# Sigmoid attention feeding a top-1 mixture of experts: the SyncE queue asks for raw weights and the last two pairs in other steps

## The chip, the cores and the metric

The kernel runs on one core of a Trainium2 chip, as one launch. The metric is the device time of the launch in microseconds (us), lower is better. A core has five engines with an instruction stream each: PE (TensorE), DVE (VectorE), ACT (ScalarE), POOL (GpSimd) and SP (SyncE). Nearly all DMAs of this kernel are issued by SP, whose queue takes them strictly in program order: where one DMA has to wait for a buffer, everything behind it on SP waits too.

## What is computed

Eight batches of 448 tokens with twelve heads of width 64 go through a sigmoid attention; its output, as 3584 token rows of 768, goes through a mixture of eight experts, of which each token takes the one with the largest gate logit.

```python
scores = scale * np.matmul(q, k.transpose(0, 1, 3, 2)) - np.log(S)
attn = 1.0 / (1.0 + np.exp(-scores))
x = np.matmul(attn, v)                    # then (B*S, H*D)
logits = x @ w_gate;  expert_idx = np.argmax(logits, axis=1)
for e in range(E):
    mask = expert_idx == e
    h = np.maximum(x[mask] @ w1[e], 0.0)
    out[mask] = gate_w[mask, None] * (h @ w2[e])
```

## The kernel before

**Attention in phases.** Heads are taken in pairs, six pairs to a batch, two pairs at a time. `attention()` runs 168 steps `s`; 21 steps (`PB`) are a phase `ph`, one batch, and `r` is the step within the phase. A step makes the scores of one seventh of two pairs (8 matmuls of L589, then two sigmoids on ACT) and the weighted sums of the step two before (8 matmuls of L604). So the two pairs whose scores begin at r = 0, 7 and 14 need their values at r = 2, 9 and 16. Pair `g` belongs to phase `g // 6`.

**Dense blocks.** Behind step r = 1 of a phase stands the expert block of batch `b = ph - 2`: all 448 tokens of the batch through the expert that most of them took (`moe`, L229 and L248, 288 matmuls). For batches 1 to 5 (`LEFT`) the block stands in an If (L786, L787) on `whole`, which says whether more than 240 tokens took that expert. Where they did not, the other arm runs, which has no matmuls. Tokens that no block covers are gathered into items at the end. In these inputs seven of the eight blocks run; the one of batch 4, at the start of phase 6, does not.

**What SP does in a late phase.** Phases 3 to 7 from r = 2 on are called `late`. There SP issues, in the order of the program:
- `vn`, the values of a pair (`load_values`, 224 KB, one DMA for an even pair, two for an odd one), into four buffers, at r = 1, 4, 8, 11, 15 and 18. The ones at r = 8, 15 and so on wait for the L604 matmuls that release a buffer;
- `wst`, raw tiles of the next block's weights (L180, 384 KB each) into a ring of five. `wts.load(n)` makes sure that n are asked for; `FIRST` holds the steps. From r = 18 (`SPLIT`) `wts.ahead` splits the first three in two parts on DVE and asks for one more raw tile for each;
- `kn` and `qn`, keys and queries of a pair (`load_pair`, L496, eight DMAs of 56 KB in runs of 128 B), into four buffers. `turn` (L559) transposes them on DVE before the scores can use them;
- `g_tok` (L413, one DMA of 448 single words to DRAM, gate letter "w" at r = 13) and its way back, `g_blocks` (L420, r = 18);
- `x_tok`, token rows of three pairs (`token_rows`, L449, four DMAs of 168 KB to DRAM), at r = 15 and r = 1, once DVE has turned them (`xt`).

In the If, both arms hold the first values, turns and loads of the next pairs (`BESIDE_LOADS`): in the arm with the block they stand between its matmuls, in the other arm one behind the other, 35 DMAs of SP with nothing between them.

All loops are unrolled and the order is the order of the code (`manual_schedule`); a step's loads of weights stand ahead of its matmuls, its `todo` behind them, then the gate steps.

Of the kernel before, what the change touches and what calls it, by code (L numbers as in the profile page):

```python
# [25 lines left out]
def tile_sigmoid_attention_top1_moe(  # L26
# [93 lines left out]
    def gate_columns():  # L120
        nc.gpsimd.tensor_copy(wgp[:, :, 0:E], wg)
# [22 lines left out]
    def raw_view(st, n):  # L144
        return st.rearrange("p (t f) -> p t f", f=n)

    def w2_rows(ereg, r, st):
        d, jh = divmod(r, 2)
        src = w2[bass.ds(ereg, 1), jh * 4 * P : (jh + 1) * 4 * P, d * DW : (d + 1) * DW]
        nc.sync.dma_start(raw_view(st, DW), src.rearrange("e (t p) f -> p (e t) f", p=P))  # L150
# [9 lines left out]
    class Weights:  # L160
# [9 lines left out]
        def load(self, n):  # L170
            while self.loaded < min(n, len(self.eregs) * self.LOADS):
                b, i = divmod(self.loaded, self.LOADS)
                ereg = self.eregs[b]()
                if ereg is None:
                    break
                st = next(raw_ring)
                if i < KF:
                    eng, ereg = (nc.gpsimd, regs["first"]) if b == 0 else (nc.sync, ereg)
                    src = w1[bass.ds(ereg, 1), :, i * P : (i + 1) * P].rearrange("e (t p) f -> p (e t) f", p=P)
                    eng.dma_start(raw_view(st[:, :DM], P), src)  # L180
                else:
                    w2_rows(ereg, i - KF, st)
                self.raw[self.loaded] = st
                self.loaded += 1
# [408 lines left out]
    def weighted(s):  # L593
# [25 lines left out]
    UB = NP // 2  # L619
    PB = UB * ST  # L620
    FIRST = {9: 1, 11: 2, 13: 3, 15: 4, 17: 5}
    SPLIT = PB - 3
    LATE = range(LEFT.start + 2, LEFT.stop + 2)
    TICK = 14
# [14 lines left out]
    LAST = {2: lambda u: load_pair(2 * u + 4), 5: lambda u: load_pair(2 * u + 5)}  # L639
# [24 lines left out]
    }  # L664
    FIRST_LAST = {2: lambda u: load_pair(2 * u + 6), 5: lambda u: load_pair(2 * u + 7)}

    BESIDE_LOADS = {
        2: lambda u: turn(2 * u + 2, "k"),
        3: lambda u: (turn(2 * u + 2, "q"), load_values(2 * u + 2)),
# [7 lines left out]
    def attention():  # L677

        order = ExitStack()
        order.enter_context(tc.manual_schedule())  # L680
        for g in range(2):
            first_pair(g)
        nc.gpsimd.dma_start(wg, w_gate.rearrange("(t p) e -> p t e", p=P))
        load_values(0)
        load_values(1)
        warm_up(WARM)
        first_turn(0)
        first_turn(1)
        for g in (2, 3):
            load_pair(g)  # L690
        for g in (2, 3):
            load_values(g)
        write_blank = blank_records()
        gate_columns()
        pend = {}

        def gate_step(b, what):
            if what == "a":
                gate_a(b)
            elif what == "b":  # L700
                pend[b] = gate_b(b)
            elif what == "c":
                pend[b] = gate_c(b, *pend[b])
                gate_out[b] = pend[b][0]
            elif what == "l":
                load_regs(b)
            elif what == "d":
                gate_d(b, *pend.pop(b))
            elif what == "p":
                put_records(b)  # L710
            elif what == "w":
                put_gates(b)
            elif what == "e":
                gate_e(b)
            elif what == "x":
                while turned:
                    token_rows(*turned.pop(0))
            else:
                for t in range(2):
                    low_half(b, 2 * what + t)  # L720

        ALONE_GATES = {
            3: "a", 4: "b", 6: (0, "c"), 7: (1, "l"), 8: (2,), 12: "d", 18: "w",
        }
        BESIDE_GATES = {
            0: "xa", 1: "b", 3: "c", 4: "l", 5: "w", 6: "d", 7: "p", 8: "e", 11: (0,), 12: (1,), 13: (2,),
        }
        FIRST_GATES = {
            1: "a", 2: "b", 4: "c", 5: "l", 7: "x", 9: "d", 10: "w", 12: (0,), 13: (1,), 14: (2,), 15: "p", 17: "e",
        }  # L730
        LATE_GATES = {
            3: "b", 5: (0, "c"), 6: (1, "l"), 7: (2,), 11: "d", 13: "w", 16: "p", 18: "e",
        }
        ALONE = 2 * PB

        for s in range(N_ST + 2):
            u, i = divmod(s, ST)
            held = ALONE <= s < ALONE + 2
            ph, r = divmod(s, PB)
            late = LATE.start <= ph < LATE.stop and r > 1  # L740
            nb = ph - 1 if late else 0
            if (late or s < ALONE) and r in FIRST and ph:
                wts.load(nb * wts.LOADS + FIRST[r])
            if (late or s < ALONE) and SPLIT <= r and ph:
                wts.ahead(nb * wts.PARTS + r - SPLIT + 1, early=True)
            if s < N_ST and not held:
                scores(s)
            if s >= 2:
                weighted(s - 2)
            if s < N_ST:  # L750
                m = u % UB
                alone = u < 2 * UB - 1
                todo = READY if u < 2 * UB - 2 else LATER if alone or u >= 2 * UB and m else {}
                if i in todo:
                    todo[i](u)
                if u >= 2 * UB and m == UB - 1 and i in LAST:
                    LAST[i](u)
                if u == 2 * UB and i in FIRST_LAST:
                    FIRST_LAST[i](u)
            for what in ALONE_GATES.get(s - PB, ()) if s < ALONE else ():  # L760
                gate_step(0, what)
            for what in LATE_GATES.get(r, ()) if late else ():
                gate_step(nb, what)
            if i in (1, 5) and not ALONE - ST < s < ALONE + 2 or s == ALONE - 5:
                gate_step(None, "x")
            if s == ALONE - 4:
                write_blank()
            elif s == ALONE - 2:
                load_pair(ALONE // ST * 2)
            b, r = divmod(s - 1, PB)  # L770
            b -= 2
            if s == ALONE:
                yield TICK
            if r or b < 0:
                continue
            if b in LEFT:
                u = UB * (b + 2)
                for g in (2, 3):
                    for nm in "kq":
                        turned_tile(2 * u + g, nm)  # L780
                    value_tile(2 * u + g)
                for g in range(2 * u + 4, min(2 * u + 8, NG)):
                    pair_tiles(g)
                rows = list(turned)
                turned.clear()
                whole = nc.values_load(gate_out[b][0:1, 1:2], min_val=0, max_val=1)  # L786
                with tc.If(whole >= 1) as whole_if, tc.manual_schedule():  # L787
                    for tick in range(14):
                        if tick == 0:
                            for at in rows:  # L790
                                token_rows(*at)
                        elif tick in BESIDE_LOADS:
                            BESIDE_LOADS[tick](u)
                        yield TICK
                    yield PER + 1 - 14 * TICK
                with whole_if.Else(), tc.manual_schedule():
                    for at in rows:
                        token_rows(*at)
                    for load in BESIDE_LOADS.values():
                        load(u)  # L800
                gate_step(b + 1, "a")
                continue
            for tick in range(0 if b else 1, 20 if b < B - 2 else 15):
                yield TICK
                for what in (BESIDE_GATES if b else FIRST_GATES).get(tick, ()):
                    gate_step(b + 1, what)
                if b == 0 and tick == 1:
                    gate_e(0)
                elif b == 0 and tick == 2:
                    put_records(0)  # L810
                todo = BETWEEN if b else FIRST_BETWEEN
                if b < B - 2 and tick in todo:
                    todo[tick](UB * (b + 2))
            if b < B - 2:
                yield PER + 1 - 20 * TICK
            if b == 0:
                for n in range(2):
                    scores(ALONE + n)
        order.close()

    wts = Weights([(lambda b=b: regs.get(b)) for b in range(B)])
# [362 lines left out]
```

## Time and profile before

| | before |
|---|---|
| median of 3 runs | 802.11 us (799.76 to 805.47) |
| the profiled execution | 798.6 us |
| its span, from the first to the last instruction | 796.9 us |
| PE busy | 771.9 us (97%) |
| DVE, ACT, POOL busy | 437.1, 376.0, 131.2 us |
| mean granted TensorE clock | 0.985 |
| DMA of SP's queue | 277070 packets, 95.96 MB, 54.1% of 16 engines |

The span is 1.7 us shorter than the time of the same execution. PE is the engine that is nearly always busy, so what matters is where it is not, and where it runs at the lower clock; the page shows both in the 40 slices of the span. Windows over a stage, the timelines of SP, PE and DVE and the chain that ended last then tell what PE waited for.

### The profile page before, as it was taken

The page shows a single profiled execution, that of the slowest core. Times are in us where ns is not written, and L with a number is a line of the kernel's source. Part 1 is how long each engine was busy: PE and PEld are TensorE (multiplying, and loading weights), DVE is VectorE, ACT ScalarE, POOL GpSimd, SP SyncE. Part 2 cuts the span into 40 slices and gives each one's busy share as a digit, 9 for nine tenths or more (in the row PEclk, how much of TensorE's full clock was granted, in tenths as well). Part 3 has the DMA queues.
Part 4 walks back from the last instruction along what each step waited for, and adds up shares of the span by engine and source line. Part 5 has one row for each costly group of instructions (what it writes and reads, how often), then busy time and mean ns, then how long its engine had stood idle before and what let it go on. Part 6 is the DMA issues. An engine that isn't in the chain of part 4 may idle for free.

```text
span 796.9 us, 15247 instructions
## 1 busy us (share of the span) xinstructions
PE 771.9 (97%) x5480; PEld 591.0 (74%) x5480; DVE 437.1 (55%) x932; ACT 376.0 (47%) x681; POOL 131.2 (16%) x201
## 2 busy tenths in 40 slices
PE   9999999999999999999999767999999999999996
PEld 5545898889964899559984323799747998999885
DVE  2475676245447644665436537354375674466763
ACT  6876333863228431573317436442283331335662
POOL 4442305000121002110031001001210223032011
PEclk9999999999999999999999889899999999999999
DMA  8968889567528884288736877884266646688211
GB/s 164 191 144 167 223 173 202 111 141 198 100 47 144 191 227 82 62 155 226 163 68 118 117 165 153 149 219 111 47 112 184 138 111 187 181 283 305 74 37 37
DMA packets 285940, 117.69 MB, mean 148 GB/s; under 512 B 204284, under 2 KB 275980, under 8 KB 285854
## 3 DMA queue, kind: packets, MB, share of 16 engines
q1 hardware_dynamic: 277070, 95.96, 54.1%
q0 software_dynamic: 8352, 19.95, 10.4%
q8 instruction: 47, 0.77, 0.4%
q10 hardware_dynamic: 432, 0.69, 0.3%
q14 instruction: 39, 0.32, 0.2%
HBM read 94.36 MB, written 22.39 MB: 147 GB/s over the span
## 4 chain that ended last, share of the span: by engine, by line
PE 89%; issue 4%; DMA 3%; SPq 2%; DVE 1%; ACT 0%; POOLq 0%; POOL 0%; DVEq 0%
PE ps L248 26%; PE ps L229 25%; PE sc L589 16%; PE av L604 15%; PE ps L1018 2%; PE ps L1046 2%; SPq L496 2%; DMA vn<-in_v_dram 1%; PE psg L284 1%; DMA x_tok<-xt 0%; SPq L449 0%; DMA wst<-in_q_dram 0%; PE pl L300 0%; PE px L950 0%; DMA qn<-in_q_dram 0%
## 5 line engine op out<-in xcount | busy, mean ns | idle before, releaser
L576 ACT ACTIVATE at<-sc,bias_s 128x448 f32<-128x448 f32 x336 | 196.2, 635 | 136.1 <-PE sc L589 133.9
L604 PE MATMUL av<-at,vn 64*64 64x448 f32 x1344 | 192.6, 545 | 5.8 <-DMA vn<-in_v_dram 5.8
L589 PE MATMUL sc<-qt,kt 64*64 64x448 f32 x1344 | 192.6, 554 | 5.4 <-DVE gsum L288 5.4
L589 PEld LDWEIGHTS sc<-qt,kt 64*64 64x64 f32 x1344 | 87.3, 189 | 62.9 <-issue 40.6
L229 PE MATMUL ps<-xh,w1h 128*128 128x448 f32 x336 | 124.2, 370 | 0.3 <-DVE hl L235 0.3
L229 PE MATMUL ps<-xh,w1l 128*128 128x448 f32 x336 | 123.5, 368 | 0.0
L248 PE MATMUL ps<-hh,w2l 128*128 128x448 f32 x336 | 123.0, 366 | 0.0
L248 PE MATMUL ps<-hh,w2h 128*128 128x448 f32 x336 | 123.0, 366 | 0.0
L229 PE MATMUL ps<-xl,w1h 128*128 128x448 f32 x336 | 122.9, 366 | 0.0
L248 PE MATMUL ps<-hl,w2h 128*128 128x448 f32 x336 | 122.8, 365 | 0.0
L604 PEld LDWEIGHTS av<-at,vn 64*64 64x64 f32 x1344 | 68.7, 136 | 67.4 <-issue 56.5
L266 POOL DMA_DIRECT2D out_dram<-ob x84 | 53.9, 649 | 359.3 <-DVE ob L261 329.4
L234 ACT ACTIVATE hh<-ps 128x448 fp32r<-128x448 f32 x56 | 30.5, 545 | 140.1 <-PE ps L229 140.1
L157 ACT CAST w2h<-wst 128x512 fp32r<-128x512 f32 x84 | 54.0, 661 | 81.1 <-PE ps L248 77.5
L158 DVE TENSOR_TENSOR w2l<-wst,w2h 128x512 fp32r<-128x512 f32 x84 | 56.7, 688 | 53.7 <-ACT w2h L157 53.7
L235 DVE SCALAR_TENSOR_TENSOR hl<-ps,hh 128x448 fp32r<-128x448 f32 x56 | 34.8, 621 | 75.6 <-ACT hh L234 75.6
L229 PEld LDWEIGHTS ps<-xh,w1h 128*128 128x128 f32 x336 | 63.1, 188 | 9.7 <-issue 3.5
L613 DVE COPY x<-av 128x448 f32<-128x448 f32 x48 | 29.0, 604 | 74.3 <-ACT xh L612 74.3
L229 PEld LDWEIGHTS ps<-xh,w1l 128*128 128x128 f32 x336 | 63.1, 188 | 6.9 <-issue 1.1
L229 PEld LDWEIGHTS ps<-xl,w1h 128*128 128x128 f32 x336 | 63.1, 188 | 5.8 <-issue 0.4
L248 PEld LDWEIGHTS ps<-hh,w2h 128*128 128x128 f32 x336 | 63.1, 188 | 5.1 <-issue 0.2
L248 PEld LDWEIGHTS ps<-hl,w2h 128*128 128x128 f32 x336 | 63.1, 188 | 5.0
(146 smaller groups left out, 830.4 us busy)
## 6 DMA issues: line engine op xcount, KB each, us to landing
wst<-in_moe_w_dram SPq DMA_DIRECT2D x50, 512.0 KB
wst<-in_moe_w_dram SPq DMA_DIRECT2D x56, 384.0 KB
x_tok<-xt SPq DMA_DIRECT2D x64, 168.0 KB
kn<-in_k_dram SPq DMA_DIRECT2D x184, 56.0 KB
qn<-in_q_dram SPq DMA_DIRECT2D x168, 56.0 KB
out_dram<-ob POOLq DMA_DIRECT2D x84, 112.0 KB, 3.3
kept<-in_moe_w_dram SPq DMA_DIRECT2D x12, 512.0 KB
vn<-in_v_dram SPq DMA_DIRECT2D x16, 224.0 KB
```

What stands on the lines that cost most here:

```text
L157: (nc.vector.tensor_copy if early else nc.scalar.copy)(hi, st)
L158: eng.tensor_tensor(lo, st, hi.bitcast(F32), op=ALU.subtract)
L229: nc.tensor.matmul(ps[:, :S], a[:, ws], b_, start=(t == 0 and n == 0), stop=(t == KD - 1 and n == 2))
L234: nc.scalar.activation(hh[:, :S], ps[:, :S], AF.Relu)
L235: nc.vector.scalar_tensor_tensor(hl[:, :S], ps[:, :S], 0.0, hh[:, :S].bitcast(F32), op0=ALU.max, op1=ALU.subtract)
L248: nc.tensor.matmul(ps[:, :S], a, b_, start=(j == 0 and n == 0), stop=(j == KF - 1 and n == 2))
L266: nc.gpsimd.dma_start(out[b * S : (b + 1) * S, cols].rearrange("(j r) f -> r j f", r=32), obv[32 * i : 32 * (i + 1)])
L496: eng.dma_start(t[32 * a : 32 * (a + 1)], src[b, 2 * hp + h, :, 32 * f : 32 * (f + 1)].rearrange("(j r) s -> r j s", r=32),)
L576: nc.scalar.activation(at, ps[:, :S], AF.Sigmoid, bias=bias_s, scale=SCALE)
L589: nc.tensor.matmul(ps[quarter(g, h), :S], ks, ops[g, "q"][OWN[h]], start=True, stop=True)
L604: nc.tensor.matmul(psv[g][OWN[h], :S], ops[g, "v"][rows, c, :], at[rows], start=(c == 0), stop=(c == KC - 1))
L613: nc.vector.tensor_copy(x, pv[:, :S])
```

## The change

In late phases the five raw tiles are asked for at r = 8, 9, 10, 11, 12 in place of 9, 11, 13, 15, 17. The last two pairs, which were loaded at r = 16 and r = 19 (`LAST` in the third group of a phase), are loaded at r = 13 and r = 15. In the other arm of the If the loop over `rows` stands behind the loads in place of ahead of them.

```diff
     FIRST = {9: 1, 11: 2, 13: 3, 15: 4, 17: 5}
+    LATE_FIRST = {8: 1, 9: 2, 10: 3, 11: 4, 12: 5}
...
+    LATE_LAST = {13: lambda u: load_pair(2 * u + 2), 15: lambda u: load_pair(2 * u + 3)}
...
-            if (late or s < ALONE) and r in FIRST and ph:
-                wts.load(nb * wts.LOADS + FIRST[r])
+            first = LATE_FIRST if late else FIRST if ph == 1 else {}
+            if r in first:
+                wts.load(nb * wts.LOADS + first[r])
...
-                if u >= 2 * UB and m == UB - 1 and i in LAST:
+                if u >= 2 * UB and m == UB - 1 and i in LAST and not late:
                     LAST[i](u)
+                if late and r in LATE_LAST:
+                    LATE_LAST[r](UB * (ph + 1))
...
                 with whole_if.Else(), tc.manual_schedule():
+                    for load in BESIDE_LOADS.values():
+                        load(u)
                     for at in rows:
                         token_rows(*at)
-                    for load in BESIDE_LOADS.values():
-                        load(u)
```

Only SP's order differs between the two programs; PE, DVE, ACT and POOL have the same instructions in the same order.

First place, SP in phase 5, around the values of pairs 35 and 36 (`vn_35`, `vn_36`); `kn2`, `qn2` are keys and queries of pair 38, `kn3`, `qn3` of pair 39, and an ISA row sets the address of the raw tile behind it. Before:

```order
L547 DMA vn_35_5108<-in_v_dram 64x448 x2
L180 ISA
L180 DMA wst1_82<-in_moe_w1_dram 128x6x128
L413 DMA g_tok_59<-gates_116 112x4x1
L180 ISA
L180 DMA wst2_83<-in_moe_w1_dram 128x6x128
L503 DMA vn_36_5202<-in_v_dram 128x448
L449 DMA x_tok_57<-xt_5_0_5047 32x14x96 x4
L496 DMA kn2_137<-in_k_dram 32x14x32 x4
L496 DMA qn2_141<-in_q_dram 32x14x32 x4
L180 ISA
L180 DMA wst3_84<-in_moe_w1_dram 128x6x128
```

Now:

```order
L180 ISA
L180 DMA wst2_83<-in_moe_w1_dram 128x6x128
L547 DMA vn_35_5110<-in_v_dram 64x448 x2
L180 ISA
L180 DMA wst3_84<-in_moe_w1_dram 128x6x128
L496 DMA kn2_137<-in_k_dram 32x14x32 x4
L496 DMA qn2_141<-in_q_dram 32x14x32 x4
L413 DMA g_tok_59<-gates_116 112x4x1
L503 DMA vn_36_5211<-in_v_dram 128x448
L496 DMA kn3_138<-in_k_dram 32x14x32 x4
L496 DMA qn3_142<-in_q_dram 32x14x32 x4
L449 DMA x_tok_57<-xt_5_0_5048 32x14x96 x4
```

The fifth raw tile (`wst3`) and pair 38 have moved ahead of `vn_36`, pair 39 ahead of the token rows; `g_tok` stands behind pair 38. The raw tiles 1 to 4 stand ahead of `vn_35`, where it was two.

Second place, SP in phase 6, behind the If, around the values of pairs 40 and 41. Before:

```order
L427 TENSOR_LOAD ri_5_6002
L427 ISA x2
L503 DMA vn_40_6092<-in_v_dram 128x448
L180 ISA
L180 DMA wst3_84<-in_moe_w1_dram 128x6x128
L180 ISA
L180 DMA wst4_85<-in_moe_w1_dram 128x6x128
L547 DMA vn_41_6144<-in_v_dram 64x448 x2
```

Now:

```order
L427 TENSOR_LOAD ri_5_6002
L427 ISA x2
L180 ISA
L180 DMA wst3_84<-in_moe_w1_dram 128x6x128
L503 DMA vn_40_6093<-in_v_dram 128x448
L180 ISA
L180 DMA wst4_85<-in_moe_w1_dram 128x6x128
L180 ISA
L180 DMA wst0_81<-in_moe_w1_dram 128x6x128
L180 ISA
L180 DMA wst1_82<-in_moe_w1_dram 128x6x128
L547 DMA vn_41_6146<-in_v_dram 64x448 x2
```

One raw tile has moved ahead of `vn_40`, and two more ahead of `vn_41`.

Third place, the whole of the other arm at the start of phase 6 in the changed program:

```order
L792 UNCONDITIONAL_BRANCH
L503 DMA vn_38_5374<-in_v_dram 128x448
L496 DMA kn0_135<-in_k_dram 32x14x32 x4
L496 DMA qn0_139<-in_q_dram 32x14x32 x4
L547 DMA vn_39_5377<-in_v_dram 64x448 x2
L496 DMA kn1_136<-in_k_dram 32x14x32 x4
L496 DMA qn1_140<-in_q_dram 32x14x32 x4
L496 DMA kn2_137<-in_k_dram 32x14x32 x4
L496 DMA qn2_141<-in_q_dram 32x14x32 x4
L496 DMA kn3_138<-in_k_dram 32x14x32 x4
L496 DMA qn3_142<-in_q_dram 32x14x32 x4
L792 UNCONDITIONAL_BRANCH
```

Before, the same rows stand there in the same order (the branches have line 787). There is no row of `x_tok` in it: the If stands behind r = 1, and the gate step "x" of that same step has already written every row that was turned, so the list `rows` is empty.

## Rows read from the trace of the kernel before

**Rows 1.** The page: span, and PE's busy time, share and instructions.

```profile
span 796.9 us, 15247 instructions
PE 771.9 (97%) x5480; PEld 591.0 (74%) x5480; DVE 437.1 (55%) x932; ACT 376.0 (47%) x681; POOL 131.2 (16%) x201
```

**Rows 2.** Windows: stretch, length, PE, PEld, DVE, ACT, POOL busy, PEclk, DMA share, GB/s.

```profile
415.53:448.40 32.87, 32.87 (x344) 16.21 (x340) 22.88 (x66) 25.54 (x48) 6.53 (x9) 1.00 0.72 103
448.40:510.48 62.08, 45.75 (x367) 21.97 (x365) 27.19 (x73) 28.10 (x52) 3.91 (x5) 0.84 0.78 149
```

**Rows 3.** Timelines of PE, then DVE: start, length, instruction, count [idle before, releaser].

```profile
451.67 1.23 PE L284 MATMUL psg<-x,wgp 128*32 128x224 f32 x12 [3.26 <-PEq L787]
...
466.95 1.02 PE L589 MATMUL sc<-qt,kt 64*64 64x448 f32 x2 [5.42 <-DVE gsum L288]
...
470.75 1.78 PE L589 MATMUL sc<-qt,kt 64*64 64x448 f32 x8
...
464.62 0.65 DVE L559 STREAM_TRANSPOSE kt<-kn 128x448 f32<-128x448 f32 x1 [8.60 <-DMA kn<-in_k_dram]
...
466.55 0.35 DVE L288 COPY gsum<-psg 128x224 f32<-128x224 f32 x1
```

**Rows 4.** The chain at the second stop, then PE's timeline behind it.

```profile
491.00 6.15 DMA vn<-in_v_dram
...
497.20 1.47 PE L604 MATMUL av<-at,vn 64*64 64x448 f32 x2 [4.66 <-DMA vn<-in_v_dram]
...
510.41 0.47 PE L229 MATMUL ps<-xh,w1h 128*128 128x448 f32 x1
```

**Rows 5.** Timeline of SP's DMA issues, phases 5 and 6.

```profile
427.93 1.67 SPq L180 DMA_DIRECT2D wst<-in_moe_w_dram  x2
...
431.59 0.48 SPq L413 DMA_DIRECT2D g_tok<-gates  x1
432.31 0.37 SPq L180 DMA_DIRECT2D wst<-in_moe_w_dram  x1
437.84 0.36 SPq L503 DMA_DIRECT2D vn<-in_v_dram  x1
439.98 2.22 SPq L449 DMA_DIRECT2D x_tok<-xt  x4
442.24 8.37 SPq L496 DMA_DIRECT2D kn<-in_k_dram  x4
450.65 3.08 SPq L496 DMA_DIRECT2D qn<-in_q_dram  x4
...
465.14 2.54 SPq L449 DMA_DIRECT2D x_tok<-xt  x4
469.12 0.36 SPq L503 DMA_DIRECT2D vn<-in_v_dram  x1
...
486.16 2.00 SPq L496 DMA_DIRECT2D qn<-in_q_dram  x4
488.87 0.35 SPq L503 DMA_DIRECT2D vn<-in_v_dram  x1
```

**Rows 6.** Windows late in phases 5, 4 and 6; columns as in rows 2.

```profile
436.30:444.30 8.00, 8.00 (x90) 4.03 (x88) 5.50 (x10) 6.68 (x13) 2.67 (x3) 1.00 0.96 46
...
343.50:349.50 6.00, 6.00 (x68) 2.93 (x67) 3.55 (x7) 5.31 (x11) 2.66 (x3) 1.00 0.88 36
497.00:504.00 7.00, 6.80 (x40) 4.58 (x44) 3.40 (x6) 2.08 (x4) 0.00 (x0) 0.54 0.81 48
```

**Rows 7.** Windows in which raw tiles and values are moved; columns as in rows 2.

```profile
427.30:436.30 9.00, 9.00 (x100) 4.40 (x99) 7.05 (x22) 7.63 (x15) 1.19 (x2) 1.00 1.03 220
...
455.00:458.00 3.00, 3.00 (x22) 1.08 (x16) 0.65 (x1) 0.00 (x0) 0.00 (x0) 0.50 1.02 257
```

**Rows 8.** Timelines in phase 4: SP's values of the odd pair, and PE where it needs them.

```profile
336.66 2.00 SPq L547 DMA_DIRECT2D vn<-in_v_dram  x2
...
345.56 0.93 PE L604 MATMUL av<-at,vn 64*64 64x448 f32 x8
```

## The prediction

> **What bounds the kernel now.** I read the page first: the span is 796.9 us and PE is busy for 771.9 us of it [rows 1]. So PE sets the time, and what a change of SP's order can win lies in the few places where PE stands still or is slow. The 40 slices of the page put the largest of them between 440 and 510 us; windows by stage then show how it differs from the rest. In phase 5, up to the If, PE is busy for the whole 32.87 us at full clock. From the end of those matmuls to the next block it takes 62.08 us for the branch and the 20 steps of phase 6, with 45.75 us busy and a mean granted clock of 0.84 [rows 2]. This is the one block that is left out: elsewhere 59 us of matmuls stand between the steps of two phases and hide every load. Here, if phase 6 took what phase 5 takes, some 29 us less would be needed.
>
> The timelines show two stops in it. The first: PE waits until 466.95 for the copy `gsum` [rows 3]. DVE makes that copy at 466.55 and had stood for 8.60 us, until 464.62, for keys, the last pair's (pair 39) [rows 3]. They are late because SP was late to ask: pair 38 begins at 442.24, and pair 39 comes behind it, two raw tiles, values and the gates' way back [rows 5]. The second stop: at step 16 PE waits for the second half of its values, pair 41, which SP asks for at 491.00 and which land 6.15 us later; PE goes on at 497.20 [rows 4]. SP's queue is the reason again. It enters the other arm at 469.12 and issues 35 DMAs without a break until 488.16 (486.16 and 2.00), at 0.50 us each, and reaches the values of pair 40 at 488.87 [rows 5]. What ends last is therefore SP's progress: arm entered, arm issued, values of pair 41. From PE's return at 497.20 to the block at 510.41 [rows 4] nothing of the change lies on the path.
>
> **The change part by part.** *The loop of the other arm.* Its list is empty, as SP's order shows. No instruction moves: 0.
>
> *The last two pairs and the fifth raw tile, in phase 5.* SP is free from 432.68 to 437.84, 5.16 us, waiting for PE to release the buffer of pair 36 [rows 5]. The eight DMAs of pair 38 and the fifth raw tile now stand ahead of that wait. From 437.84 to the arm at 469.12 SP needs 31.28 us for 35 DMAs [rows 5]; 26 are left. What goes is pair 38, from 442.24 to 453.73 (450.65 and 3.08), 11.5 us, and a raw tile's issue, 0.37 us: 11.9 us at most [rows 5]. But eight DMAs of a pair need only 4.0 us at 0.50 each; the other 7.5 us of those 11.5 SP was held up, and pair 39, which moves into that place, may be held up in its stead. Then only 4.4 us go. These are the two ends.
>
> To choose, I look at what held SP up. `g_tok` is issued at 431.59 [rows 5]. Until 436.3 the queue moves 220 GB/s [rows 7]; then, for 8 us, 46 GB/s at a DMA share of 0.96, so the engines are occupied and little arrives. Phases 4 and 6 have the same stretch, 36 and 48 GB/s for 6 and 7 us [rows 6]. I take it for the effect of the 448 single words of `g_tok`. Now a raw tile and pair 38 go ahead of `g_tok`: 384 KB at 257 GB/s [rows 7] is 1.5 us, and 4.0 us for the pair, 5.5 us, less what the first raw tile gains by being asked for before 427.93. I estimate that the slow stretch ends 4 us later, at 448.3. Of pair 39 four or five DMAs will have been taken by then. Some 21 are left (three or four of pair 39, eight of token rows, three raw tiles, two of values, four of the gates), at 0.52 us with the gap 10.9 us, and the branch takes 1.44 us (467.68 to 469.12) [rows 5]. SP enters the arm at 460.6, **8.5 us earlier**, between the ends 4.4 and 11.9.
>
> *The raw tiles of phase 6.* The arm itself is unchanged. Behind it one raw tile moves ahead of the values of pair 40, and four stand ahead of those of pair 41, where it was two: two are new. Their issue alone is 2 x 0.37 = 0.7 us [rows 5]; if their data go first, it is 2 x 1.53 = 3.1 us at 257 GB/s and 3.6 at 220 [rows 7]. The values of pair 41 took 6.15 us to land with the two raw tiles and the values of pair 40 just ahead of them [rows 4, 5], so they do stand behind data. I take **3.1 us lost**, ends 0.7 and 3.6. The Trainium skill, "DMA: Bandwidth & Descriptors", section "Queues, rings and completion order", says that each DMA engine takes descriptors in the order of its ring. By that rule the two tiles go first whole, and the gain is 8.5 - 3.1; with the issue alone it would be 8.5 - 0.7 = 7.8 us. The trace agrees as far as the 6.15 us go; no row separates the two.
>
> *PE's first stop.* It goes with pair 39's earlier keys, but wins nothing of its own. If only the 5.42 us of rows 3 went, PE would stand at step 16 at 487.1 in place of 492.5 (497.20 less 4.66 [rows 4]), still ahead of the values of pair 41 at 497.15 - 8.5 + 3.1 = 491.8. The gain of the first stop becomes wait in the second. Behind it the clock stays as it is: 0.54 granted in 497 to 504 [rows 6], which is the lower level, 1.2 GHz, for nearly all of it, after a stop of 4.66 us; the new stop is no shorter.
>
> *Phases 3, 4, 5 and 7 elsewhere.* Every load is hidden by PE's steps and blocks [rows 2], so earlier raw tiles and pairs win nothing: 0. What they cost if that cover is too thin is a rival.
>
> **The sum:** 8.5 - 3.1 = 5.4 us. The profiled execution took 798.6 us, 1.7 more than its span, which gives 793.2; it lies 3.5 us below the median of the runs, 802.11, so the forecast of the median is 802.1 - 5.4 = **796.7 us**. The ends of the terms give 4.4 - 3.6 = 0.8 and 11.9 - 0.7 = 11.2 us, 801.3 and 790.9.
>
> **Rivals.** *Held up all the same (801.3, chance 0.22).* Pair 39 meets the slow stretch where pair 38 met it, SP wins 4.4 us, and the raw tiles take 3.6 back. For it: SP has to push 8 DMAs of 448 short runs into a queue that stands. Against: fewer DMAs are left behind the stretch than before. The HBM Reference of the Trainium skill, section "Latency", gives 0.2 us for an access on average and 2 us at high load. By that rule the slow stretch would come from load, and five tiles and a pair at once would lengthen it. The rows do not bear it out: the highest rates, 220 and 257 GB/s, run without it [rows 7], and phase 4, with less queued, has it too [rows 6].
>
> *No hold-up (790.9, chance 0.20).* SP pushes pair 39 through, or the stretch is over sooner; then all 11.9 us go, and the two tiles cost little because the slow `g_tok` of phase 6 now stands further behind pair 41 (in the old order it was one raw tile behind).
>
> *Values late in every phase (slower, chance 0.08).* The values of an odd pair stand behind four raw tiles, where it was two. In phase 4 they are asked for at 336.66 and needed at 345.56 [rows 8], 8.9 us. With the 6.15 us of phase 6 [rows 4] and 3.1 us for two more tiles they would come after 9.25 us: it decides when the landing grows by over 2.8 us. Then PE stops in phases 3, 4, 5 and 7, for up to 2 us each and, if its clock falls as in 497 to 504 (0.54 over 7 us [rows 6]), 3.2 us more: four times 5.2 less the 5.4 won is +15, 817 us; with only two phases hit, 807. Against it: the first tile is asked for earlier, in time in which SP now waits for PE, which gives most of it back.
>
> **How the numbers follow.** The forecast, 3 to 8 us won, has 0.50. Faster or slower is told at 1%, 8 us, about what a measurement of this kernel can tell from no change: faster needs a time under 794.1. All of the no-hold-up case is there and about 0.08 of the forecast's upper edge: 0.28. Slower by 8 us needs three phases hit: 0.06. The rest, 0.66, is within 1%. The range 790.0 to 802.5 takes in both ends of the sum and leaves out about 0.1 above and less below.
>
> **What would show it.** Right: pair 38 issued before 437.8 or held up only shortly; the arm entered near 460.6 on SP; no wait of `gsum` for keys; one stop of PE, 8 to 10 us long, at step 16 of phase 6, that ends with the values of pair 41 some 5 us earlier than now. The slow stretch should follow `g_tok` to its new place. Wrong: the arm entered after 465 (held up), the stop at step 16 gone (then I have misjudged the tiles), or a new stop of L604 for values in phases 3, 4, 5 or 7.

## The result and the profile after

The changed kernel takes 806.47 us in the median of 20 runs (804.06 to 809.27), the kernel before 801.96 us in 20 runs beside them. The ratio is 1.0055, with a 95% interval of 1.0042 to 1.0068: by it 4.4 us slower, where 5.4 us of gain were forecast. The profiled execution took 804.16 us. Its page answers to [rows 1]:

```profile
span 802.4 us, 15256 instructions
PE 775.2 (97%) x5480; PEld 601.9 (75%) x5480; DVE 437.4 (55%) x932; ACT 377.7 (47%) x681; POOL 131.1 (16%) x201
```

The two stretches of [rows 2], from step 2 of phase 5 to the If and from there to the next block, in the changed kernel (columns as there):

```profile
418.93:453.42 34.49, 34.31 (x344) 18.07 (x340) 23.03 (x66) 26.27 (x49) 6.66 (x10) 1.00 0.62 112
453.42:514.67 61.25, 43.73 (x365) 23.59 (x365) 27.37 (x73) 28.49 (x51) 3.78 (x4) 0.83 0.71 144
```

The second is 0.8 us shorter than before; the first, which had no idle time, is 1.6 us longer. The same 1.6 to 2 us are lost at steps 15 to 17 of phases 3, 4 and 7 too. It would be wrong to explain the result by that. From which chips these two traces come is not on record, and on one chip all traces, two of the kernel before and two of the changed one, lose 1.3 to 2.7 us at this place in each of the four phases (up to the last L604 matmul, against [rows 1]'s trace). From here on traces of that one chip are compared (before: spans of 803.6 and 802.3 us; changed: 806.5 and 806.4).

Windows of the kernel before on that chip: steps 14 to 17 of phase 5, from 18 to the last sigmoids ahead of the If, the way into the If up to `psg`, from there to step 4, to step 15, to the block. Columns as in [rows 2].

```profile
440.18:447.33 7.15, 6.56 (x70) 3.40 (x65) 3.49 (x7) 5.26 (x10) 3.02 (x4) 1.00 1.24 61
447.33:453.08 5.75, 5.75 (x68) 4.81 (x64) 4.59 (x7) 4.78 (x9) 0.00 (x0) 1.00 0.90 128
453.08:456.13 3.05, 1.17 (x12) 0.19 (x5) 1.43 (x3) 2.02 (x4) 0.13 (x1) 1.00 0.52 92
456.13:477.48 21.35, 11.58 (x70) 3.84 (x74) 4.68 (x13) 2.43 (x4) 0.00 (x0) 0.68 0.74 172
477.48:497.76 20.28, 18.30 (x194) 8.28 (x186) 12.90 (x46) 13.68 (x27) 3.79 (x4) 1.00 0.62 110
497.76:514.91 17.15, 13.73 (x105) 7.94 (x105) 8.08 (x13) 10.64 (x19) 0.00 (x0) 0.80 1.20 173
```

The same pieces of the changed kernel:

```profile
440.42:448.30 7.88, 7.39 (x68) 3.54 (x64) 2.37 (x5) 5.36 (x11) 3.03 (x4) 1.00 0.90 95
448.30:454.07 5.77, 5.77 (x68) 4.85 (x64) 5.67 (x9) 4.79 (x9) 0.00 (x0) 1.00 0.78 43
454.07:460.28 6.21, 1.17 (x13) 0.19 (x5) 3.98 (x8) 2.02 (x5) 0.13 (x1) 0.90 0.54 67
460.28:472.44 12.16, 10.34 (x70) 4.59 (x74) 1.93 (x7) 2.32 (x5) 0.00 (x0) 0.63 0.79 209
472.44:490.58 18.14, 17.81 (x180) 9.99 (x176) 12.48 (x46) 14.31 (x27) 0.18 (x1) 1.00 0.67 125
490.58:518.62 28.04, 15.42 (x122) 9.52 (x114) 9.18 (x14) 11.03 (x19) 3.60 (x4) 0.76 0.74 134
```

The way into the If grew from 3.05 to 6.21 us, the piece behind `psg` shrank by 9.2, and the last pieces, with the second stop, grew by 8.8. From step 14 to the block it is 74.7 us before and 78.2 after; the second trace of each has 75.3 and 78.5. In the mean that is 3.3 us of the 3.5 by which the times of these four executions differ. What PE waited for, in its timeline before and then changed:

```profile
456.13 0.95 PE L284 MATMUL psg<-x,wgp 128*32 128x224 f32 x12 [1.88 <-PEq L787]
472.39 1.02 PE L589 MATMUL sc<-qt,kt 64*64 64x448 f32 x2 [5.87 <-DVE gsum L288]
497.96 0.97 PE L604 MATMUL av<-at,vn 64*64 64x448 f32 x4 [2.18 <-DMA vn<-in_v_dram]
502.15 1.56 PE L604 MATMUL av<-at,vn 64*64 64x448 f32 x2 [3.22 <-DMA vn<-in_v_dram]
```

```profile
460.28 1.71 PE L284 MATMUL psg<-x,wgp 128*32 128x224 f32 x12 [5.04 <-PEq L792]
499.89 1.76 PE L604 MATMUL av<-at,vn 64*64 64x448 f32 x4 [7.24 <-DMA vn<-in_v_dram]
507.03 1.22 PE L604 MATMUL av<-at,vn 64*64 64x448 f32 x2 [5.38 <-DMA vn<-in_v_dram]
```

The first stop (`gsum`, [rows 3]) is gone. The second ([rows 4]) consists of two waits in these traces: the first ends with the values of pair 40 (issued at 494.77 before, at 496.63 in the changed kernel), the second with those of pair 41 (issued from 497.90 and 499.30). Together they went from 5.4 to 12.6 us, and PE resumes 66.6 us behind step 14 (507.03 less 440.42) where it was 62.0. So the second stop ends last, as before, and it is set by SP. SP's timeline (as in [rows 5]) before, then changed:

```profile
436.63 0.48 SPq L413 DMA_DIRECT2D g_tok<-gates  x1
447.30 8.24 SPq L496 DMA_DIRECT2D kn<-in_k_dram  x4
455.59 3.05 SPq L496 DMA_DIRECT2D qn<-in_q_dram  x4
474.44 0.36 SPq L503 DMA_DIRECT2D vn<-in_v_dram  x1
494.77 0.17 SPq L503 DMA_DIRECT2D vn<-in_v_dram  x1
497.90 1.12 SPq L547 DMA_DIRECT2D vn<-in_v_dram  x2
```

```profile
443.64 0.48 SPq L413 DMA_DIRECT2D g_tok<-gates  x1
446.11 3.69 SPq L496 DMA_DIRECT2D kn<-in_k_dram  x4
450.76 8.92 SPq L496 DMA_DIRECT2D qn<-in_q_dram  x4
474.11 0.37 SPq L503 DMA_DIRECT2D vn<-in_v_dram  x1
496.63 0.48 SPq L503 DMA_DIRECT2D vn<-in_v_dram  x1
497.38 1.81 SPq L180 DMA_DIRECT2D wst<-in_moe_w_dram  x3
499.30 3.36 SPq L547 DMA_DIRECT2D vn<-in_v_dram  x2
```

Pair 39 now takes 13.6 us (446.11 to 459.68) behind `g_tok`, where pair 38 took 11.3. The arm is entered 33.7 us behind step 14 in place of 34.3. From the arm's entry to the end of the second stop it is 32.9 us in place of 27.7. These two lengths are used below for every trace.

### The profile page after: what moved, and what is told of

It is laid out like the page before. It is cut to its first block, busy times and chain, and to the rows that moved or that the text cites. A ratio compares the mean times of both kernels' runs of the same rounds, so it can differ in the third digit from the quotient of the medians.

```text
span 802.4 us, 15256 instructions
## 1 busy us (share of the span) xinstructions
PE 775.2 (97%) x5480; PEld 601.9 (75%) x5480; DVE 437.4 (55%) x932; ACT 377.7 (47%) x681; POOL 131.1 (16%) x201
## 5 line engine op out<-in xcount | busy, mean ns | idle before, releaser
L604 PE MATMUL av<-at,vn 64*64 64x448 f32 x1344 | 206.9, 543 | 12.0 <-DMA vn<-in_v_dram 12.0
L589 PE MATMUL sc<-qt,kt 64*64 64x448 f32 x1344 | 204.6, 551 | 1.1 <-ACT at L576 1.1
L589 PEld LDWEIGHTS sc<-qt,kt 64*64 64x64 f32 x1344 | 95.6, 189 | 56.9 <-issue 33.0
L604 PEld LDWEIGHTS av<-at,vn 64*64 64x64 f32 x1344 | 75.9, 134 | 69.1 <-issue 47.5
```

The lines of the kernel that those rows point to most:

```text
L589: nc.tensor.matmul(ps[quarter(g, h), :S], ks, ops[g, "q"][OWN[h]], start=True, stop=True)
L604: nc.tensor.matmul(psv[g][OWN[h], :S], ops[g, "v"][rows, c, :], at[rows], start=(c == 0), stop=(c == KC - 1))
```

## The experiments

The table has, for each kernel, the ratio to the kernel before in runs on the same chip, the time from step 14 of phase 5 to SP's entry into the arm ("arm"), from there to the end of PE's second stop ("stop"), and the way into the If, from the start of the last two sigmoids to `psg` ("If"), all three in us from its trace. A trace is one execution: those of numbers 1 and 2 are the slowest of their ten runs (807.81 and 808.49 us, medians 802.49 and 803.44), that of number 9 is the fastest of its five (790.66, median 792.17).

| kernel | `g_tok` | tiles ahead of the values of pair 41 | last pairs | ratio (95%) | arm | stop | If |
|---|---|---|---|---|---|---|---|
| before, three traces | words | 2 | late | 1 | 33.5, 34.3, 34.9 | 28.1, 27.7, 27.4 | 4.0, 3.1, 3.8 |
| changed, four traces | words | 4 | early | 1.0055 (1.0042-1.0068) | 31.3, 33.1, 33.7, 34.2 | 32.1, 31.9, 32.9, 32.1 | 3.9, 7.5, 6.2, 6.8 |
| 1: tiles alone | words | 4 | late | 1.0031 (1.0008-1.0053) | 33.4 | 30.7 | 3.7 |
| 2: pairs alone | words | 2 | early | 1.0043 (1.0015-1.0071) | 35.7 | 30.1 | 8.7 |
| 3: two tiles ahead | words | 2 | early | 1.0017 (0.9991-1.0043) | 34.3 | 27.9 | 5.1 |
| 4: five tiles ahead | words | 5 | early | 1.0112 (1.0071-1.0154) | 31.0 | 32.8 | 6.3 |
| 5: values first | words | 0 | early | 1.0024 (1.0004-1.0045) | 37.0 | 23.8 | 5.6 |
| 6: changed, 16 B | 112 runs | 4 | early | 0.9993 (0.9975-1.0011) | 30.2 | 32.1 | 2.7 |
| 7: before, 16 B | 112 runs | 2 | late | 0.9950 (0.9930-0.9969) | 31.5 | 27.5 | 3.5 |
| 8: before, 128 B | 16 runs | 2 | late | 0.9982 (0.9963-1.0000) | 34.2 | 27.7 | 5.8 |
| 9: values first, 128 B | 16 runs | 0 | early | 0.9906 (0.9873-0.9940) | 30.9 | 23.4 | 3.9 |
| 10: values first, old pairs, 128 B | 16 runs | 0 | late | 0.9944 (0.9926-0.9962) | 37.8 | 23.2 | 10.0 |
| 11: changed, 128 B | 16 runs | 4 | early | 0.9970 (0.9948-0.9992) | 29.2 | 32.0 | 3.8 |
| 12: gates ahead of the pairs | words | 4 | early | 1.0065 (1.0038-1.0093) | 32.8 | 36.7 | 4.5 |
| 13: gates late, old order | words | 2 | late | 1.0242 (1.0199-1.0285) | 41.1 | 27.7 | 3.4 |

### 1 to 4: the two halves, and more or fewer tiles ahead of the values

My first theory, V, took the loss in phases 3, 4, 5 and 7 for the change's.

```diff
# 1: raw tiles alone
-if u >= 2 * UB and m == UB - 1 and i in LAST and not late:
+if u >= 2 * UB and m == UB - 1 and i in LAST:
-if late and r in LATE_LAST:
-    LATE_LAST[r](UB * (ph + 1))
# 2: pairs alone
+LATE_FIRST = {9: 1, 11: 2, 13: 3, 15: 4, 17: 5}
# 3: two tiles ahead of the odd pair's values
+LATE_FIRST = {8: 1, 9: 2, 12: 3, 13: 4, 14: 5}
# 4: five tiles ahead
+LATE_FIRST = {8: 1, 9: 2, 10: 3, 11: 5}
```

> The raw tiles of the change alone (r = 8 to 12); the last two pairs stay at r = 16 and r = 19. The changed kernel (806.5 us) loses about 1.6 us at steps 15 to 17 of each of phases 3, 4, 5 and 7 and gains nearly nothing in phase 6. If the values of the odd pair, which stand behind four raw tiles in place of two, cause that loss (theory V), it stays here whole, phase 6 keeps its first stop for keys, and its second stop, for the values of pair 41, grows by about 3 us: 808 to 812 us. If the early pairs cause it (theory P: eight DMAs of short runs ahead of the values at r = 15), phases 3, 4, 5 and 7 run as before the change and only phase 6 loses up to 3 us: 802 to 805.

> The early pairs of the change alone (r = 13 and r = 15); the raw tiles stay at r = 9, 11, 13, 15 and 17. Theory V: no loss in phases 3, 4, 5 and 7, the first stop of phase 6 goes, and without the two more tiles ahead of the values of pair 41 the second ends 4 to 8 us earlier: 794 to 798 us. Theory P: the loss of 1.6 us in each of the four phases stays: 800 to 804.

> The changed kernel with the raw tiles at r = 8, 9, 12, 13, 14: two of them stand ahead of the odd pair's values, as before the change, and all five are still asked for earlier than before. Theory V: the steps 15 to 17 of phases 3, 4, 5 and 7 run without loss, and phase 6 gains 4 to 8 us: 794 to 798 us. Theory P: the loss stays, 800 to 806.

> The changed kernel with the suspected cause made larger: all five raw tiles ahead of the odd pair's values (r = 8, 9, 10, 11, 11). Theory V: the values come about 1.5 us (one tile of 384 KB) later still, so the loss in phases 3, 4, 5 and 7 grows from 1.6 to about 3 us each and the second stop of phase 6 by 1.5: 811 to 815 us. Theory P: as the changed kernel in phases 3, 4, 5 and 7, 1.5 us more in phase 6: 806 to 808.

Neither theory held: both halves are slower by themselves. The four traces show nothing at steps 15 to 17 in 14 of their 16 phases, so the 1.6 us of the first trace do not belong to the order. Two phases do stop for values, and badly: phase 3 of number 1 loses 7 us, and phase 7 of number 4 loses 5.7. In number 1 PE waits here, and on SP a raw tile and `g_tok` stand right behind the values (issued from 244.41 to 246.49):

```profile
258.44 0.98 PE L604 MATMUL av<-at,vn 64*64 64x448 f32 x1 [4.40 <-DMA vn<-in_v_dram]
```

```profile
247.23 1.26 SPq L413 DMA_DIRECT2D g_tok<-gates  x1
```

The packets of these values run from 247.8 to 252.3; in the trace of before they ended by 248.4, when most of the single words had yet to come. Values are late, as in the rival *Values late*, but only in two of the eight phases of numbers 1 and 4, and the four tiles ahead are not shown to be the reason: PE goes on at 258.44, 6 us behind the last of these packets.

### The kernels again, for the spread

> The changed kernel once more, nothing edited, for a second trace of it. If the order itself costs the steps 15 to 17 of phases 3, 4, 5 and 7 (theory V, the values behind four raw tiles), each of the four shows a loss of 1 to 2 us there again, and the time is 4 to 5 us above the kernel before. If it is a matter of what happens to meet in the queue (theory S, the slow stretch behind the single words of g_tok catches whatever is queued there), some of the four phases are clean and others lose more, up to 7 us as phase 3 did with the raw tiles alone.

It lost nothing at steps 15 to 17 of phases 3, 4 and 5, 3.5 us on the way into the If, 2.4 in phase 7: theory S rather than V. Later two more traces of either kernel, on one chip, gave the comparison of the first section:

> The kernel before, nothing edited, for a second trace of it. If its order is safe from the stretch (two raw tiles ahead of the odd pair's values, pair 38 in the stretch), phases 3, 4, 5 and 7 have no stop at steps 15 to 20 again, and the way into the If costs about 3 us as in the first trace. If stops there are accidents of any order, at least one of the four phases loses over 1 us.

> The kernel before once more, a third trace: as the run ahead of it.

> The changed kernel, nothing edited, a third trace. Two traces of it lost 1.6 us in each of phases 3, 4, 5 and 7, and 0, 0, 3.5 (on the way into the If) and 1.8 us. If that is what the order costs, phases 3, 4, 5 and 7 lose 3 to 7 us together again, in changing places, and phase 6 gains 0 to 1.5 us on the first trace of before.

> The changed kernel once more, a fourth trace: as the run ahead of it.

Both traces of before lost 1.6 to 2.1 us in phases 3, 4 and 7 and 1.3 in phase 5, so those stops are no effect of the order. The changed kernel's own loss is the 3.3 us from step 14 of phase 5 to the block.

### 5: the values ahead of all raw tiles

```diff
-LATE_FIRST = {8: 1, 9: 2, 10: 3, 11: 4, 12: 5}
+LATE_FIRST = {12: 1, 13: 2, 14: 3, 15: 4, 16: 5}
```

> The changed kernel with all five raw tiles behind the odd pair's values: r = 12, 13, 14, 15, 16 in place of 8 to 12; the pairs stay at r = 13 and 15. Theory V: phases 3, 4, 5 and 7 lose nothing at steps 15 to 17, and in phase 6 the values of pair 41 are asked for right behind the arm: 3 to 6 us faster than before. Theory S: the values are safe here too, but pair 39, the token rows and the way into the If still stand in the slow stretch, so phase 5 loses 2 to 5 us ahead of the block and the sum stays within 2 us of before.

The time is what theory S expected, within 2 us of before. "Stop" fell from 32 to 23.8 us, but the arm came 2 us later than in any trace of before, and phase 7 lost 3.9 us in its block, where PE waited for VectorE.

### 6 and 7: the same gates in 112 runs of 16 B

```diff
-nc.sync.dma_start(g_tok[b].rearrange("(c p) -> p c", p=CP), gates[:CP, b])
+nc.sync.dma_start(g_tok[b].rearrange("(p c) -> p c", p=CP), gates[:CP, b])
```

> The changed kernel with g_tok written as 112 runs of 16 B in place of 448 single words: the same bytes, but in another order, so the gates that are read back belong to other tokens and the output differs. Theory S, in the form that the number of single words makes the stretch: it shrinks from 6 to 10 us to 2 us or less, pair 39 is issued in about 4 us, the other arm is entered 8 to 10 us earlier than before, no stop falls into steps 15 to 17: 6 to 10 us faster than before. Theory V: the loss at steps 15 to 17 stays, and the time is 2 to 5 us above before. If the stretch has nothing to do with g_tok: as the changed kernel, 4 to 5 us above before.

> The kernel before with the same edit of g_tok (112 runs of 16 B, gates of other tokens). Theory S: pair 38 is issued in 4 to 5 us in place of 11.5, the wait of 8.6 us of VectorE for the keys of pair 39 goes, the other arm is entered some 7 us earlier: 4 to 7 us faster than before. If the stretch has nothing to do with g_tok: no difference, within 1 us.

The shape of this one write is worth 4.0 us in the old order (4 to 7 were expected) and some 5 in the new one, by two ratios from different sets of runs. Number 6 itself is 0.6 us faster than before, where 6 to 10 were expected, and its interval holds 1. Pair 38 of the old order, 11.5 us long in [rows 5], now takes 8.4, and the arm is entered at 467.91:

```profile
442.88 5.37 SPq L496 DMA_DIRECT2D kn<-in_k_dram  x4
448.29 2.99 SPq L496 DMA_DIRECT2D qn<-in_q_dram  x4
```

So the words do hold SP up, which the prediction only took for granted, but they are only a part of it: 8.4 us is still twice the 4.0 that eight DMAs take where nothing holds them. Windows of the kernel before, then of number 7 (columns as in [rows 2]), show where the words count: from 434 to 440 the DMA share is higher with them and the rate lower, from 446 to 452 there is no difference.

```profile
434.00:440.00 6.00, 6.00 (x72) 2.93 (x68) 1.88 (x4) 5.17 (x10) 3.86 (x4) 1.00 1.28 106
446.00:452.00 6.00, 2.74 (x36) 1.48 (x31) 3.19 (x5) 3.17 (x6) 0.13 (x1) 1.00 0.79 106
```

```profile
434.00:440.00 6.00, 6.00 (x72) 2.93 (x68) 1.76 (x6) 4.96 (x11) 3.55 (x4) 1.00 0.89 142
446.00:452.00 6.00, 3.18 (x40) 1.28 (x36) 3.63 (x7) 3.73 (x8) 0.13 (x1) 1.00 0.80 107
```

In the changed order "arm" falls to 30.2 us, but "stop" stays at 32.1, so their sum, 62.2 us, is that of the kernel before (61.6 to 62.3).

### 8 to 11: the gates in rows

VectorE transposes the tile of all gates, and SyncE writes 16 runs of up to 128 B in four DMAs.

```diff
+nc.vector.memset(gates, 0.0)                                   # once, at the start
-nc.sync.dma_start(g_tok[b].rearrange("(c p) -> p c", p=CP), gates[:CP, b])
+nc.vector.transpose(turned_gates, gates.rearrange("p b c -> p (b c)"))
+to = g_tok[b].rearrange("(c p) -> c p", p=CP)
+for k in range(4):
+    w, at = min(32, CP - 32 * k), 32 * k + NCH * b
+    nc.sync.dma_start(to[:, 32 * k : 32 * k + w], turned_gates[at : at + NCH, :w])
# 8: in the kernel before   11: in the changed kernel
# 9, 10: with LATE_FIRST as in 5; 10 with the pairs back to r = 16 and 19
```

> The kernel before, with g_tok written in 16 runs of up to 128 B: VectorE first transposes the tile of all gates, then SyncE issues four DMAs of four partitions each in place of one of 448 single words. The result is the right one here. Theory S: no slow stretch, so the gain of the 112 runs of 16 B in the same order (4 us) comes again, less up to 1.5 us for three more DMAs on SyncE in each phase: 3 to 5 us faster than before. If it was the wrong order of the gates and not the shape of the write that helped there: no gain.

> The same g_tok in the changed kernel, with the five raw tiles behind the odd pair's values (r = 12 to 16) and the pairs at r = 13 and 15. Theory S together with the tiles' price: phases 3, 4, 5 and 7 lose nothing, the way into the If costs 2 to 3 us, the first stop of phase 6 is gone and the second ends when the values of pair 41, asked for right behind the arm, land: 6 to 9 us faster than before. If the tiles ahead of the values of pair 41 cost little (0.7 us, their issue alone), it is no faster than the same g_tok with the changed kernel's tiles, 0 to 2 us faster than before.

> As the run before, but the last two pairs stay at r = 16 and r = 19. If the early pairs have a use of their own once the stretch is gone, this is slower than the run before by 1 to 4 us: the copy gsum waits for the keys of pair 39 for 3 to 5 us again. If the second stop swallows that, as step 16 did in my sum, the two are equal within 1 us.

> The changed kernel with its own tiles and pairs and the new g_tok. By what 112 runs of 16 B gave there: 0 to 1 us faster than before, since phases 3, 4, 5 and 7 are clean and the arm is entered earlier, but four raw tiles stand ahead of the values of pair 41, which land as late as before (near step 16 plus 12 us of stops). Against the same with the values first it is slower by 6 us or more if the tiles go ahead of the values whole, by 1 us if only their issue counts.

Number 9 beats both kernels: 792.17 us, by its ratio 7.5 us less than before. Against 11, which differs in the tiles alone, it wins 5.1 us, and against 10, which differs in the pairs alone, 3.0 (4.2 by the medians). The tiles' price is seen in SP's and PE's timelines of 11, then 9:

```profile
487.07 0.49 SPq L510 DMA_DIRECT2D vn<-in_v_dram  x1
487.83 1.66 SPq L181 DMA_DIRECT2D wst<-in_moe_w_dram  x3
489.60 3.01 SPq L554 DMA_DIRECT2D vn<-in_v_dram  x2
```

```profile
497.03 1.35 PE L611 MATMUL av<-at,vn 64*64 64x448 f32 x2 [4.91 <-DMA vn<-in_v_dram]
```

```profile
487.09 0.35 SPq L510 DMA_DIRECT2D vn<-in_v_dram  x1
487.54 1.13 SPq L554 DMA_DIRECT2D vn<-in_v_dram  x2
```

```profile
489.96 2.09 PE L611 MATMUL av<-at,vn 64*64 64x448 f32 x7 [4.86 <-DMA vn<-in_v_dram]
```

The values of pair 41 (L554) are issued 2.1 us earlier, and PE goes on 7.1 us earlier. But it is not the same wait that ends last: in 11 it is the one for pair 41, 7.4 us behind their issue, in 9, as in 5 and 10, the one for pair 40 (L510), 2.8 us behind theirs. Over the table "stop" is 23.2 to 23.8 us with no tile ahead, 27.4 to 28.1 with two (30.1 in number 2), 30.7 to 32.9 with four or five (36.7 in number 12). From two to four that is 1.5 us (number 1) to 2.5 us for a tile; the fifth shows nothing more in "stop", and with none pair 40 sets the end. In time, with the words and the early pairs, none, two, four and five tiles ahead give the ratios 1.0024, 1.0017, 1.0055 and 1.0112. Number 8 gained 1.4 us, with an interval that reaches 1, less than the 3 to 5 expected: rows in place of words are not all of it, and in its one trace pair 38 still took 10.9 us.

### 12 and 13: the place of `g_tok`

```diff
# 12: changed kernel
-11: "d", 13: "w", 16: "p", 18: "e"
+11: "d", 12: "w", 16: "p", 18: "e"
# 13: kernel before
+11: "d", 16: "pw", 18: "e"
```

> The changed kernel with g_tok at r = 12 in place of 13, so that its single words stand ahead of pairs 38 and 39 again, where they were before. Theory W (the early pair pushes g_tok's slow stretch 7 to 10 us later, onto pair 39 and onto the way into the If): the stretch begins at its old place, the way into the If is short again (from the block of batch 3 to psg 96 to 97 us, where three of four traces of the changed kernel have 99.7 to 100.2), phase 6 keeps 58 to 59 us because of the raw tiles: 0 to 1 us above the kernel before. If it is the early pairs themselves (16 DMAs of short runs ahead of the branch): 99 us or more again, 3 to 5 us above the kernel before.

> The kernel before with g_tok at r = 16, behind the token rows and pair 38, in place of r = 13: the same shift of its single words without the early pairs or tiles. Theory W: the stretch now lies on the last two steps and the way into the If: 98 to 101 us from the block of batch 3 to psg, where three traces of the kernel before have 96.2 to 96.9, and 2 to 4 us above the kernel before in time. If the early pairs themselves are the cause: no difference there, within 1 us of the kernel before.

Theory W fails as I put it. In 12 the way into the If is short (4.5 us), yet the kernel is no faster than the changed one. In phase 6 the values of pair 41 come late and in two pieces; the words now stand close behind them, which fits, but no run shows that they are the reason:

```profile
505.65 1.75 PE L604 MATMUL av<-at,vn 64*64 64x448 f32 x2 [4.79 <-DMA vn<-in_v_dram]
509.06 1.01 PE L604 MATMUL av<-at,vn 64*64 64x448 f32 x1 [1.67 <-DMA vn<-in_v_dram]
```

"Stop" is 36.7 us, the longest of all. In 13 `g_tok` reached SP's head only at 461.35, behind `psg`, so it says nothing on the way into the If. What it does show: its way back waits for it until 469.91, everything of SP stands behind that, "arm" is 41.1 us, and other stretches lose as well (behind the last attention step 8.8 us against [rows 1]'s trace).

## Why the prediction was wrong

**What bounds the kernel: right.** The second stop ends last and SP sets it. The changed kernel's loss is the sum of the two lengths that the prediction added up: "arm" 34.6 to 34.0 us and "stop" 27.5 to 32.5 in the means of the two traces each on one chip, so PE resumes 4.3 us later. The first stop went and won nothing of its own, as the text said: the 9.2 us by which the piece behind `psg` shrank came back as 8.8. How long the second stop becomes is told twice in the prediction, and not alike: its times for step 16 make 4.7 us (491.8 less 487.1), its signs say 8 to 10. Measured are 12.6. Its 0.50 us for a DMA of the arm is the issue alone; 35 in 19.04 us are 0.54 each, which changes nothing in the sum.

**The arm, 8.5 us earlier: mis-sized, and the larger miss.** It is entered 0.6 us earlier on the same chip (1.1 in the means of all seven traces). Pair 38 did go out early (437.44 to 443.59) into SP's idle time, and the slow stretch did follow `g_tok`. But the estimate that the stretch ends 4 us later, with four or five DMAs of pair 39 taken and the rest at 0.52 us, failed: SP spent 13.6 us on pair 39 and 7.6 us on the eight token-row DMAs (4.6 in the trace of before). The window of 448.30 to 454.07 moves 43 GB/s where before moves 128. That is beyond the end I called *Held up all the same* (4.4 us). Even without the words the arm comes 3 to 5 us earlier (numbers 6, 9 and 11), so none of them reaches 8.5.

**The tiles, 3.1 us: mis-sized, outside its ends.** Two more tiles cost 5.0 us on the chip compared ("stop" 32.5 less 27.5) and 4.3 in number 11 against 8. I priced a tile by its bytes at the highest rates of [rows 7], 1.53 us, and took its issue for the other choice; the two add up. On that chip the values of pair 41 take 7.5 us from issue to landing, before 4.1, and are issued 25.0 us behind the arm's entry, before 23.4: 3.4 and 1.6 us. Number 11 against 8 has 2.7 and 1.6, the first trace of the changed kernel against [rows 4]'s 0.8 and 3.2, so the split varies. The 1.6 us hold more than the 0.7 of two issues: the arm's last four DMAs were held up (3.23 us, before 1.99), and the value DMAs too (3.36 us for two, before 1.12).

The two sizes turn a gain of 5.4 us into 0.6 less 5.0, a loss of 4.4. The runs have 4.4 us, the four executions traced on that chip 3.5. These have 4.3 us of it at the end of the second stop; 1.0 comes back up to the block, and phase 3 is 0.5 longer; the rest lies elsewhere.

**Phases 3, 4, 5 and 7, cost 0: right in the kernel as changed**, within 0.6 us in the means on one chip. The rival *Values late in every phase* did not decide it, though values did come late in single phases of numbers 1 and 4.

**The way into the If: not in the prediction at all.** It grew by 3.1 us on the same chip. It does not add to the sum, since PE waits longer later in any case: number 10 has the longest way, 10.0 us, and is 4.5 us faster than before.

**What stays open:** why a pair is slow where no words are (pair 38 takes 10.9 us in number 8 and 13.3 in number 10, pair 39 takes 10.4 in number 9), and what PE does at steps 15 to 17 in the traces that lose time there (numbers 12 and 13, from another chip than the four compared, lose 1.3 to 2.1 us there too).

## What to carry to other kernels

When one queue sets the end, moving a load forward helps only as far as what it is moved past is not itself held up: look for the transfer that stalls the queue (here, in part, one write of 448 single words) and change its shape before the order. Put the loads that are waited for next ahead of large transfers that are wanted much later, and price each such transfer by how much it delays the issue and the landing in a trace, not by bytes over the best rate. Compare traces from the same chip, and take a second one, before a difference of 1 or 2 us is put down to a change.

## What the hardware showed that I had not expected

**PE waits for its code at a branch.** The wait named PEq ahead of `psg` ends 1.5 us behind a packet of 16 KB on the instruction queue. Part 3 of the view on DMA, in the window from the last sigmoids to `psg` (packets, MB, share of 16 engines), before and changed:

```profile
q8 instruction: 1, 0.02, 3.2%
```

```profile
q8 instruction: 1, 0.02, 2.7%
```

These are 1.54 us of 3.05 and 2.64 us of 6.21. In 19 of 20 traces `psg` starts 1.46 to 1.55 us after the end of such a packet (1.80 in the other), and the packet took 0.96 to 5.0 us. It is not all of the wait: in number 10, with the longest way, 10.0 us, it took 1.28. The Trainium skill, "Runtime: NRT & Kernel Launch", section "Instruction fetch mechanics", says that a taken branch to code that has not been fetched waits for a DMA of it; the traces agree, as far as this timing goes.

**The shape of one small write moves the whole kernel.** 1.8 KB in single words or in runs of 16 B: 4.0 us of 800, in the same place and with the same bytes (number 7).
